# An S4 convolution and GeGLU block on one core: one product for the y tables, weight reads and stores moved, dummy matmuls, another instruction order

## The chip, the cores and the metric

The kernel runs on one core of a Trainium2 chip. The metric is the device time of one execution in microseconds. Three runs of the kernel before gave 823.56, 824.63 and 826.21 us (median 824.63). A separate profiled execution is the source of all trace numbers.

TensorE (PE) multiplies matrices from SBUF into PSUM, VectorE (DVE) and ScalarE (ACT) do elementwise work, and SyncE (SP), ScalarE and GpSimd (POOL) issue DMA transfers. Every engine works through its own instructions strictly in order.

## The reference

All sizes are fixed: 2048 tokens, 448 channels, 256 states per channel, 1792 hidden units.

```python
mod = (_silu(c) @ w_mod).reshape(c.shape[0], 6, 1, -1)
sa, ca, ga, sb, cb, gb = ...
h = _layernorm(x) * (1 + ca) + sa
x = x + ga * _A_ref(h, ...)          # S4 convolution
h = _layernorm(x) * (1 + cb) + sb
x = x + gb * _B_ref(h, ...)          # (gelu(h @ w_gate) * (h @ w_up)) @ w_down
# in _A_ref:
P = jnp.exp(logdA[:, :, None] * l[None, None, :])
K = jnp.einsum("dn,dnl,dn->dl", Cc, P, dB).real
y = irfft(rfft(K) * rfft(u))         # padded to twice the length
y = y + u * Dskip
```

## The kernel before, in words

**Kernel generation and convolution.** The convolution kernel K has 2048 positions for each of 448 channels, each a sum over 256 states of a complex exponential. A position is split into 64 * l1 + l2 (32 values of l1, 64 of l2). For each of 56 steps, 8 channels at a time, small bf16 matmuls with the constant tables `ea` and `rd` form exponents and angles in PSUM. ScalarE turns them into magnitudes (`exps`, tiles `mx` for l1 and `my` for l2) and into sines and cosines (`angles`, tile `fg`, in turns, with a bias tile `halfpi`). VectorE multiplies magnitude and sine or cosine (`mults`): the x factor `tx` in one instruction of 1024 columns (L855), the y factor `ty` in three: the cosine part of 1024 columns (L859), the negated sine part for one half of the l2 values (L862, 512 columns) and the sine part for the other half (L863, 512 columns). TensorE contracts `tx` and `ty` over the states (`kgen`, L886, 64 small matmuls a step). `ktail` evacuates and does the first stage of a Fourier transform (L911).

The input is normalised, transformed in two stages through DRAM (L1040, L1103), multiplied in the frequency domain with the transform of K and transformed back. Channels are taken in three groups (160, 160, 128). `k_fft` handles the first two while kernel generation still runs (L1194, L1198, L1205); `t_fft` the third after the last step (L1276 forward, L1282 and L1285 products, L1292 inverse). The results go to DRAM (L1300) and come back as rows of tokens: early rows of the first two groups (`yi_early`, L1351), last rows of the third (L1362, L1374).

**The passage.** `conv_out` finishes the convolution with small matmuls (L1466 for the early rows, L1471 for the last), adds the residual, computes mean and root (L1478, L1498), normalises (L1512, L1513) and transposes 128 tokens at a time by matmuls with an identity (L1518, L1520). ScalarE copies the result to fp16 (`ht`), VectorE subtracts for the low half (L1528). Four sets of 128 tokens make a block of 512.

**The MLP.** Four blocks. `weight` reads half a weight chunk (512 KB) from `in_wgu` (L1399) and splits it into two fp16 parts (ScalarE L1407, VectorE L1411 and L1412) in a ring of three tiles `wr`; the split chunk is also stored to DRAM (L1421) for the later blocks, which only read it back (`w_load`). The first three of seven chunks belong to the start of the first block (`PRE = 3`). `gate_up` makes the gate and up products of 128 hidden units (20 matmuls at L1594 and four at L1588), gelu on ScalarE (L1601), the product and the fp16 split; it has two pairs of PSUM banks (`pq`). In the first block the first four products are done in two halves of 256 tokens, so that they can start with two of the four sets. `down_first` and `down` make the down product (L1663, L1694, L1754) and store the output.

**Order.** Nothing runs in the order of the source. `Plan.add` records tasks with their engines, planned costs, dependencies and buffers. `Plan.order` then simulates the engines: it takes the engine that could start something first and there the task with the lowest value, either the task's own `v` or a number from the table `PRIO`. Some tasks may go to one of two engines (copies: ScalarE or VectorE), the one that ends first. `HOP` is the planned hand-over time between engines, `RATE` the planned DMA rate, one stream for all queues. The instructions are then written out in this order and stay in it on each engine.

```python
z = add("tys", {"DVE": 1.2}, s - 0.4, fs, [si, y], (), [fb, yb, ty])
...
gate = EV["end"] if cb < PRE else CO[0][1]
hold = [YO[2, 1]] if cb + k < 2 and cb < 2 else YL
t1 = add("w.ld", {"SP": 0.42}, v - 3, ld, [EV["end"]] + hold, [wb], kb=540)
```

`YO[2, 1]` is the store of the second part of the third group; `YL` are all loads of the last rows.

## Time and profile before

| what | value |
|---|---|
| runs | 823.56, 824.63, 826.21 us |
| profiled execution | 822.29 us |
| its span, first to last instruction | 820.5 us |
| TensorE busy | 744.8 us (91%) |
| VectorE busy | 609.2 us (74%) |
| ScalarE busy | 464.4 us (57%) |
| mean granted TensorE clock | 0.972 |
| DMA traffic | 136.78 MB, mean 167 GB/s |

Busy shares are means over stages with different limits; the tables by windows part them. In a row of a timeline or of the chain, the first number is the start in us from the first instruction, the second the duration; a bracket at the end tells how long the engine was idle before it and what ended that. L numbers are lines of the kernel.

### The profile page before, as it was taken

To read this page: it belongs to the slowest core of one execution; us is meant where nothing else is said; L and a number is where in the kernel's file an instruction comes from. 1 tells how busy PE (TensorE), PEld (TensorE's weight loads), DVE (VectorE), ACT (ScalarE), POOL (GpSimd) and SP (SyncE) were. 2 spreads that over 40 slices of the span, in tenths; PEclk is the share of its full clock that TensorE was granted. 3 is DMA by queue.
4 is the path that set the end of the run, shared out by engine and by line. 5 is a ranking of instruction groups with operands and counts; after the bars stand their busy time and mean duration, and the time that the engine had idled before them with its cause. 6 is when DMAs were issued, how large, how long until landed. Compare 5 with 4: busy or idle time off the path is not lost.

```text
span 820.5 us, 19136 instructions
## 1 busy us (share of the span) xinstructions
PE 744.8 (91%) x8172; PEld 455.8 (56%) x8172; DVE 609.2 (74%) x1034; ACT 464.4 (57%) x610; POOL 11.1 (1%) x28
## 2 busy tenths in 40 slices
PE   0787788989899999988689999999999999999997
PEld 0333344443577766678566445444496445954477
DVE  5799999898989999996875783178884655744552
ACT  4598998999899999880245551034332233223320
POOL 1000000000000000001200000000000000000000
PEclk9879999999999999999879999999999999999999
DMA  9644459997967755989769641644416232012101
GB/s 266 161 147 138 116 145 246 282 261 234 221 198 223 224 160 165 295 276 279 242 224 310 234 158 63 162 150 139 135 53 185 77 127 96 24 68 90 45 13 35
DMA packets 92839, 136.78 MB, mean 167 GB/s; under 512 B 22672, under 2 KB 75184, under 8 KB 92754
## 3 DMA queue, kind: packets, MB, share of 16 engines
q1 hardware_dynamic: 86480, 131.02, 52.6%
q10 hardware_dynamic: 5458, 3.12, 1.3%
q8 instruction: 64, 1.05, 0.5%
q0 software_dynamic: 816, 1.42, 0.5%
q14 instruction: 21, 0.17, 0.1%
HBM read 100.42 MB, written 36.01 MB: 166 GB/s over the span
## 4 chain that ended last, share of the span: by engine, by line
PE 62%; ACT 14%; DVE 9%; DMA 8%; issue 5%; SPq 2%; ACTq 0%; DVEq 0%
PE pq L1594 30%; PE pq L1694 8%; PE pd L1663 4%; ACT fg L819 3%; PE kg L886 3%; DMA u_d<-so 2%; PE pg L806 2%; ACT my L793 2%; PE pq L1588 2%; PE pf L1205 2%; PE pf L1103 2%; PE pd L1694 1%; DMA fg<-in_w_mod 1%; DVE ty L859 1%; ACT fg L811 1%
## 5 line engine op out<-in xcount | busy, mean ns | idle before, releaser
L1594 PE MATMUL pq<-ht,wr 128*128 128x512 f16 (+1 forms) x1200 | 248.7, 365 | 0.0
L1594 PEld LDWEIGHTS <-wr 128*128 128x128 f16 x1200 | 114.4, 98 | 128.9 <-issue 12.3
L1608 DVE TENSOR_TENSOR fq<-ge,pq 128x512 f32<-128x512 f32 (+1 forms) x60 | 39.0, 651 | 83.4 <-PE pq L1594 58.5
L1601 ACT ACTIVATE ge<-pq 128x512 f32<-128x512 f32 (+1 forms) x60 | 34.0, 567 | 113.8 <-PE pq L1588 69.4
L1620 ACT ACTIVATE hh<-fq 128x1024 f16<-128x1024 f32 (+1 forms) x49 | 47.2, 964 | 59.9 <-DVE fq L1608 44.5
L886 PE MATMUL kg<-ty,tx 128*32 128x64 f32 x3584 | 63.6, 224 | 13.4 <-DVE ty L863 9.0
L886 PEld LDWEIGHTS kg<-ty,tx 128*32 128x32 f32 x3584 | 54.4, 112 | 32.7 <-DVE ty L863 14.0
L855 DVE TENSOR_TENSOR tx<-mx,fg 128x1024 f32<-128x1024 f32 x56 | 67.3, 1215 | 2.8 <-ACT fg L830 2.8
L1694 PE MATMUL pq<-d,hh 128*128 128x224 f16 x476 | 69.3, 259 | 0.0
L859 DVE TENSOR_TENSOR ty<-my,fg 128x1024 f32<-128x1024 f32 x56 | 67.9, 1216 | 1.7 <-ACT fg L823 1.7
L1694 PE MATMUL pq<-d,hlo 128*128 128x224 f16 x238 | 61.6, 259 | 0.0
L819 ACT ACTIVATE fg<-pg 128x1024 f32<-128x1024 f32 x56 | 57.7, 1032 | 3.5 <-issue 1.5
L793 ACT ACTIVATE my<-pg 128x1024 f32<-128x1024 f32 x56 | 55.9, 1037 | 5.6 <-PE pg L788 5.1
L1623 DVE TENSOR_TENSOR hlo<-fq,hh 128x1024 f16<-128x1024 f32 (+1 forms) x49 | 53.6, 1103 | 3.1 <-ACT hh L1620 3.1
L1694 PEld LDWEIGHTS <-hh 128*128 128x128 f16 x560 | 53.9, 98 | 0.8 <-issue 0.3
L1205 PE MATMUL pf<-q,fc 128*128 128x160 f32 x264 | 41.8, 307 | 0.2
L806 PEld LDWEIGHTS <-lt 64*128 64x128 bf16 x336 | 19.3, 94 | 40.0 <-issue 26.0
L1205 PEld LDWEIGHTS pf<-q,fc 128*128 128x128 f32 x264 | 36.6, 190 | 6.2 <-issue 3.4
L806 PE MATMUL pg<-ea,lt 64*128 64x512 bf16 x168 | 33.1, 387 | 6.7 <-ACT fg L819 5.2
L863 DVE TENSOR_TENSOR ty<-my,fg 128x512 f32<-128x512 f32 x56 | 38.2, 682 | 0.0
L862 DVE SCALAR_TENSOR_TENSOR ty<-my,fg 128x512 f32<-128x512 f32 x56 | 38.1, 681 | 0.0
L911 PE MATMUL kg<-ak,ke 128*64 128x128 f32 x448 | 30.6, 279 | 3.7 <-issue 2.0
(198 smaller groups left out, 1207.2 us busy)
## 6 DMA issues: line engine op xcount, KB each, us to landing
wr<-w_d SPq DMA_DIRECT2D x21, 896.0 KB, 4.6
fc<-in_k_fc SPq DMA_DIRECT2D x20, 576.0 KB, 5.2
u_d<-so SPq DMA_DIRECT2D x32, 224.0 KB, 4.5
w<-in_wgu SPq DMA_DIRECT2D x14, 512.0 KB, 4.1
ui<-u_d SPq DMA_DIRECT2D x10, 672.0 KB, 6.2
w_d<-wr SPq DMA_DIRECT2D x7, 896.0 KB, 7.1
fq<-in_wd SPq DMA_DIRECT2D x14, 448.0 KB, 3.8
us<-uo SPq DMA_DIRECT2D x22, 240.0 KB, 6.5
```

Source lines behind the costliest of these rows:

```text
L793: A.activation(yb.tile.rearrange("p a b c -> p (a b c)"), pb.tile, AF.Exp)
L806: T.matmul(pa[:, nh * 512:nh * 512 + 512], w, x, start=(k == 0), stop=(k == 2))
L819: A.activation(fb.tile[:, 0].rearrange("p x (n k) -> p n x k", n=2), pb.tile.rearrange("p (n x k) -> p n x k", n=2, x=2), AF.Sin, scale=TW ...
L855: V.tensor_mul(tx.tile, xb.tile[:, xm, None, :].to_broadcast([128, 2, 512]), fb.tile[:, :, 0])
L859: V.tensor_mul(ty.tile[:, 1], yb.tile, fy()[:, 1, :, None, :].to_broadcast([128, 16, 2, 32]))
L886: T.matmul(kg[32 * g:32 * g + 32, 2 * (s % 2) + q, :64], tx[:, r, nh, 4 * q + g], ty[:, r, nh, 4 * q + g], start=(r == 0 and nh == 0), sto ...
L1205: T.matmul(pz.tile[:, e % 32 - sl0], fc.tile[:, i, 1 + t], pp.tile[:, t, i], start=(t == 0 and e != 32), stop=(t == 1 and e != 0))
L1594: T.matmul(pb.tile[k][:, ts], wr.tile[:, 4 * lo + t, k, c0:c0 + 128], ht[:, m, ts], start=f % 2 == 0 and i == 0, stop=f % 2 == 1 and i == 9)
L1608: V.tensor_mul(to if half is None else to[:, half:half + 1], *src)
L1620: A.activation(hg.tile[0][:, cb, c], fq.tile[:, c], AF.Copy)
L1623: V.tensor_sub(hg.tile[1][:, cb, c], fq.tile[:, c], hg.tile[0][:, cb, c])
L1694: T.matmul(bank(k)[:, m], x[:, p, q[0], ts], w[:, p, q[1]], start=new and m == 0 and p == 0 and z == 0, skip_group_check=True, stop=i in ( ...
```

## The change

- **One y product.** `ea`, `rd` and the constant `k_one` are changed so that the angles of x and y are shifted by an eighth of a turn and the l2 values lie in two halves. The four products (two halves, sine and cosine) are then plain ones, all done by one VectorE instruction of 2048 columns; the negation goes. `kgen` picks two of the four for each of its two sums, as two runs of 32 columns. The bias and scale of the cosine change sign; ScalarE writes `my` in another order.
- **Weights.** The reads of both halves of the first chunk and of one half of the second (`w.le`) wait only for the end of the kernel generation's buffers and for the load of the residual rows, and come ahead of the row loads on SyncE. The other three (`w.la`) and the stores of the first three chunks (`wr.sa`) are issued by ScalarE and wait for the first root of `conv_out`. Reads of the later four chunks stay on SyncE, behind the last `w.la`.
- **Dummy matmuls** (`spin`), two of 512 columns a task, whose results nobody reads: 5, 5, 4 and 1 tasks after kernel steps 51 to 54 (once the last angles are done), and 18 after the last copies of the third group. Their priority value is 9000, higher than any other, so that they are placed where TensorE has nothing else to start.
- **New order.** Another `PRIO`; a table `PACE` that scales planned costs; hand-over times by pair of engines; a separate planned DMA stream for each issuing queue; some kinds of tasks kept in their own sequence (`INTURN`).

```diff
+PACE = {("anc", "PE"): 0.97, ("ang", "PE"): 0.87, ("bn", "DVE"): 1.12, ...}
-PRIO = {...}
+PRIO = {...}
+    HOPD, HOPB = 0.25, 0.15
+    HOPS = {("PE", "ACT"): 0.2, ("PE", "DVE"): 0.2, ("ACT", "DVE"): 0.04, ...}
+    INTURN = ("ang", "tx", "tyc", "x.mm", "y.mm", "x.exp", "y.exp", "f.ut", ...)
...
-        def fc_():
-            ty.tile = tab.tile([128, 2, 16, 2, 32], FT, name="ty")
-            V.tensor_mul(ty.tile[:, 1], yb.tile, fy()[:, 1, :, None, :].to_broadcast([128, 16, 2, 32]))
-
-        def fs():
-            V.scalar_tensor_tensor(ty.tile[:, 0, :, 0], yb.tile[:, :, 0], -1.0, fy()[:, 0], op0=OP.mult, op1=OP.mult)
-            V.tensor_mul(ty.tile[:, 0, :, 1], yb.tile[:, :, 1], fy()[:, 0])
+        def fy():
+            ty.tile = tab.tile([128, 2, 2, 512], FT, name="ty")
+            V.tensor_mul(ty.tile, yb.tile[:, :, None, :].to_broadcast([128, 2, 2, 512]),
+                         fb.tile[:, None, :, 1].to_broadcast([128, 2, 2, 512]))
...
-                                     ty[:, r, nh, 4 * q + g], start=(r == 0 and nh == 0), stop=(r == 1 and nh == 1),
+                                     ty[:, 0:4:3, nh, 4 * q + g] if r else ty[:, 1:3, nh, 4 * q + g], start=(r == 0 and nh == 0), stop=(r == 1 and nh == 1),
...
+    def spin(n, deps, buf, first, tile_, ops):
+        for k in range(n):
+            def go(k=k):
+                if k == 0:
+                    buf.tile = tile_()
+                w, x, o = ops(buf.tile)
+                for _ in range(2):
+                    T.matmul(o, w, x, start=True, stop=True)
+            first = add("spin", {"PE": 0.43}, 9e3, go, deps + [first], [] if k else [buf], [buf] if k else [])
+        return first
+    SPIN = []
+    for s in range(NSUB - 4, NSUB):
+        SPIN.append(spin((5, 5, 4, 1)[s - NSUB + 4], [FG[NSUB - 1][1], FG[NSUB - 1][2]], Buf("pg"), KGT[s - 1], ...))
...
+        early = cb + k < 2 and cb < 2
-            dma(wb.tile, a["wgu"][cb, :, k])
+            (dma if early or cb >= PRE else adma)(wb.tile, a["wgu"][cb, :, k])
-        hold = [YO[2, 1]] if cb + k < 2 and cb < 2 else YL
-        t1 = add("w.ld", {"SP": 0.42}, v - 3, ld, [EV["end"]] + hold, [wb], kb=540)
+        if early:
+            t1 = add("w.le", {"SP": 0.42}, -1350 + k + 2 * cb, ld, [EV["end"], t_x], [wb], kb=540)
+        elif cb < PRE:
+            t1 = add("w.la", {"ACT": 0.1}, -1350 + k + 2 * cb, ld, [CO["rt", 0]], [wb], kb=540)
+            WT["la"] = t1
+        else:
+            t1 = add("w.ld", {"SP": 0.42}, v - 3, ld, [EV["end"], WT["la"]] + YL, [wb], kb=540)
...
-            dma(w_d[cb], W[0, cb].tile)
+            (adma if cb < PRE else dma)(w_d[cb], W[0, cb].tile)
...
+    spin(18, [EV["ps"], c_ih], Buf("pq"), None, lambda: POOLS["ps"].tile([128, 512], FT, name="pq0"),
+         lambda t: (K2["ih"], K2["ih"][:, None].to_broadcast([128, 4, 128]), t.rearrange("p (a b) -> p a b", b=128)))
```

## The prediction, made before the changed kernel ran

> **What bounds the kernel now.** I read the page's first line, then the busy time of each engine by stage (a table of windows: length, busy time of PE, PEld, DVE, ACT, POOL with instruction counts, then granted clock, DMA share, GB/s), because the mean over the span mixes stages with different limits.

> ```profile
> span 820.5 us, 19136 instructions
> 0.00:41.00 41.00, 17.53 (x48) 8.41 (x50) 27.02 (x66) 21.63 (x33) 3.13 (x14) 0.91 0.76 214
> 41.00:369.60 328.60, 293.79 (x5207) 182.78 (x5208) 310.15 (x489) 303.55 (x387) 0.00 (x0) 0.97 0.71 208
> 369.60:419.70 50.10, 38.07 (x362) 33.46 (x351) 37.09 (x71) 8.97 (x15) 7.94 (x14) 0.83 0.77 238
> 419.70:816.20 396.50, 395.39 (x2574) 231.10 (x2572) 234.18 (x409) 130.23 (x176) 0.00 (x0) 1.00 0.37 120
> ```

> The reader is to see four stages. Start-up (41 us) waits mostly for loads. In the kernel generation and FFTs (328.6 us) VectorE is busy 94.4% and ScalarE 92.4%: two engines bind together, and TensorE has 34.8 us free. In the passage to the MLP (50.1 us) no engine is full, so there a chain of latencies decides. In the MLP (396.5 us) TensorE is busy all but 1.1 us at full clock: nothing that the change touches can shorten it. All gain has to come from the second and third stages.

> How good can the second stage be? Two 50 us stretches of it, the loosest and the tightest:

> ```profile
> 150.00:200.00 50.00, 46.29 (x680) 21.42 (x676) 45.62 (x79) 47.13 (x70) 0.00 (x0) 1.00 0.94 275
> 250.00:300.00 50.00, 48.76 (x899) 36.46 (x900) 48.36 (x70) 48.00 (x55) 0.00 (x0) 1.00 0.66 194
> ```

> The mean of VectorE and ScalarE is 92.8% in the first and 96.4% in the second; over the whole stage it is (310.15 + 303.55) / 2 / 328.6 = 93.4%.

> The third stage I read in the chain of waits that ended last:

> ```profile
> 400.33 0.61 ACT lh L585
> 400.96 3.19 DMA y<-lh
> 404.17 0.65 SPq L1362
> 404.92 3.90 DMA w<-in_wgu
> 413.30 1.65 PE pt L1518 x6
> 419.36 0.41 PE pt L1520 x4
> 419.77 2.29 PE pq L1594 x20
> 424.68 0.67 PE pt L1518 x6
> 425.35 0.37 PE pt L1520 x4
> ```

> The last channel group's result is stored, read back as rows, added, normalised, transposed three times, and only then the first gate matmul starts, at 419.77. Look at 404.92: the rows were issued at 404.17 by SyncE (L1362), a gate weight load directly behind them, and the profile names that load as the one that came last. And look at the transposes: six matmuls take 1.65 us at 413.30, 0.67 us at 424.68. The windows say why (the last three columns again are clock, DMA share, GB/s):

> ```profile
> 400.00:403.00 3.00, 2.28 (x15) 0.79 (x13) 2.85 (x7) 2.22 (x3) 0.60 (x1) 1.00 0.96 301
> 403.00:406.00 3.00, 0.00 (x0) 0.00 (x0) 2.92 (x6) 0.38 (x1) 1.70 (x3) 0.96 0.36 94
> 406.00:409.00 3.00, 0.12 (x2) 0.15 (x4) 1.37 (x3) 0.00 (x0) 0.00 (x0) 0.50 0.92 270
> 416.00:418.00 2.00, 2.00 (x11) 1.45 (x11) 1.75 (x4) 0.39 (x2) 0.00 (x0) 0.50 0.00 0
> ```

> TensorE stops at about 402.3 (2.28 us of work from 400 on), keeps its clock for some 3.5 us (a mean of 0.96 over 403 to 406 puts the fall near 405.8), and then does all of the transposes at half clock.

> **The change part by part.** *One y product.* Each of 56 steps has three VectorE instructions (1024, 512 and 512 columns) and gets one of 2048. The busy times overlap, so starts have to be compared, not durations:

> ```profile
> 282.59 1.21 DVE L859 TENSOR_TENSOR ty<-my,fg 128x1024 f32<-128x1024 f32 x1
> 283.72 1.21 DVE L1198 TENSOR_TENSOR q<-q,pf 128x480 f32<-128x480 f32 x2
> 285.99 0.68 DVE L862 SCALAR_TENSOR_TENSOR ty<-my,fg 128x512 f32<-128x512 f32 x1
> 286.59 0.68 DVE L863 TENSOR_TENSOR ty<-my,fg 128x512 f32<-128x512 f32 x1
> 287.19 0.68 DVE L862 SCALAR_TENSOR_TENSOR ty<-my,fg 128x512 f32<-128x512 f32 x1
> ```

> A 1024-column product holds VectorE for 283.72 - 282.59 = 1.13 us, a 512-column one for 0.60. So 512 columns more cost 0.53, and 2048 cost 1.13 + 2 x 0.53 = 2.19 (at most 2 x 1.13 = 2.26). Before it is 1.13 + 0.60 + 0.60 = 2.33. That saves 0.14 us a step (0.07 at least), 56 x 0.14 = 7.8 us of VectorE (3.9 at least). [...]

> The sines and exponentials keep their shapes (a bias sign, another order of writing): 0. The kernel-generation matmuls read the same 64 columns as two runs of 32; no row shows such a read, TensorE's 34.8 free us could cover 0.62 us a step, and I take 0.

> Is 7.8 us on the path? Only half is VectorE's own: many small copies may go to either engine, so the saving is shared. Busy means fall from 306.85 to (302.35 + 303.55) / 2 = 302.95; at the stage's own 93.4% that makes 324.4 us, a gain of 4.2. If ScalarE alone holds the stage, it is 0; if VectorE alone does, 7.8.

> *New order.* Other planned costs, hand-over times and priorities reorder every engine. No row prices that. The stage could reach its tightest stretch (302.95 / 0.964 = 314.3, a gain of 14.3 with the merge) or fall to its loosest (302.95 / 0.928 = 326.5, a gain of 2.1). I take a third of the way from 93.4 to 96.4%, 94.4%: 320.9 us, a **gain of 7.7** for the stage with the merge; both ends, and the 0 of ScalarE, stay for the range. For start-up and the MLP I take 0; start-up's bound is -2 to +4, a tenth of the 41 us at most.

> *Dummy matmuls.* 18 pairs of 512 columns may run after the last group's copies (400.94), 15 pairs among the last four kernel steps. Their price and the shortened path:

> ```profile
> 445.07 4.42 PE pq L1594 x20
> 413.94 0.69 DVE L1513 SCALAR_TENSOR_TENSOR xn<-xn,rs,rows 128x448 f32<-128x448 f32 x1
> 415.32 0.69 DVE L1513 SCALAR_TENSOR_TENSOR xn<-xn,rs,rows 128x448 f32<-128x448 f32 x1
> 415.62 0.60 ACT L585 ACTIVATE ht<-pt 128x512 f16<-128x512 f32 x1 [2.43 <-PE pt L1520]
> 416.25 0.69 DVE L1528 TENSOR_TENSOR ht<-pt,ht 128x512 f16<-128x512 f32 x1 [0.25 <-ACT ht L585]
> ```

> One costs 0.22 us, so 18 pairs last 8.0 us: with the row products between them they reach from 402.3 to about 411, and the idle time that is left stays under the 3.5 us after which the clock fell. Then a transpose set takes 0.67 + 0.37 = 1.04 us. The second norm ends at 414.63, its set at 415.7, its copy (0.60) at 416.35; VectorE is free of the third norm at 416.0 and does two subtractions of 0.69, until 417.35. That is where the first gate matmul can start: **2.4 us** earlier, bound by VectorE now (bounds 0 to 2.4). A real matmul behind a pair waits up to 0.44 us; the 15 early pairs (6.6 us if all lay on the path) go into TensorE's gaps, and I take 0 for them.

> *Weight loads and stores.* The first three reads move ahead on SyncE, past the early rows and the last constants, right behind the residual rows' load; the other three and three stores leave SyncE and are issued by ScalarE behind the first root. GpSimd's row loads stay.

> ```profile
> yi<-y POOLq DMA_DIRECT2D x6, 32.0 KB, 2.7
> DMA packets 8946, 17.92 MB, mean 249 GB/s; under 512 B 1269, under 2 KB 5781, under 8 KB 8939
> 372.86 11.29 SPq L1351 DMA_DIRECT2D yi<-y  x4
> 376.89 0.69 DVE L1282 TENSOR_TENSOR q<-my,pf 128x512 f32<-128x512 f32 x1 [2.15 <-DMA fg<-in_k_fc]
> 387.90 0.69 DVE L587 COPY lh<-pf 128x512 f32<-128x512 f32 x1 [0.90 <-PE pf L1292]
> 389.24 0.69 DVE L1282 TENSOR_TENSOR q<-my,pf 128x512 f32<-128x512 f32 x1 [0.45 <-PE pf L1276]
> SPq L1399 <- DVE wr L1412: 10.6, 2, 9.8
> SPq L1421 <- DVE wr L1412: 8.0, 2, 7.1
> 389.27 5.65 ACTq L1362 DMA_DIRECT2D yi<-y  x2
> 400.96 0.37 ACTq L1300 DMA_DIRECT2D y<-lh  x1
> ```

> With no weights behind them the last rows should land like GpSimd's, 2.7 us after issue, not about 4.0: **1.3 us** (0 to 1.3). SyncE also stood 11.29 us at the early rows with the constants for the last groups queued behind them; VectorE's holes at 376.89, 387.90 and 389.24 sum to 3.5 us on the chain, and another order may fill them: I take half, **1.75** (0 to 3.5). Against it, the early reads put 1.57 MB in front of those constants, 6.3 us at 249 GB/s; the queue stands there anyway, so I take **-0.5** (0 to -6.3). Six issues of 0.37 us on ScalarE, which is busy 8.97 of 50.1 us in the stage: 0. A store by ScalarE adds a wait: behind it stand the copies, splits and gelus of the first gate products, and TensorE has two pairs of banks before it must wait for a gelu. SyncE stood 10.6 and 8.0 us at exactly those waits for VectorE's splits; freed of them, it only fetches later weights sooner, which full TensorE doesn't need: 0. If the planner places each store behind its split, ScalarE doesn't wait either: 0, up to 18.6.

> Third stage: 2.4 + 1.3 + 1.75 - 0.5 = **5.0**. Sum: 7.7 + 5.0 = 12.7 us.

> **Rivals.** *The order takes most of the idle time.* For it: the 250 to 300 stretch shows 96.4%. Against: buffers and table loads differ by stretch. Then 14.3 + 2.4 + 1.3 + 3.5 + 4 (start-up) = 25.5 us.

> *ScalarE holds the second stage.* For it: 92.4% busy with nothing removed from it. Against: copies can move. Then only 5.0 us are gained; if the early reads cost their 6.3 as well, the change does nothing that can be measured.

> *The clock falls again before the transposes.* The 18 pairs would have to be over by about 409.8, 3.5 us ahead of 413.3; if a third of them run at once in front of the rows, they are. Then the 2.4 us are lost. [...]

> *Slower: ScalarE stands at the stores.* If the order puts stores ahead of their splits, ScalarE stands like SyncE did (and like its own 5.65 us at 389.27), gelus come late, and TensorE, the bound from 419.7 on, loses each of these microseconds. In full: 18.6 us lost against 12.7 won. It decides from 15.2 us on (12.7, and 2.5 for 0.3%).

> **How the numbers follow.** The profiled execution took 822.29 us, 1.79 more than its span; the median shown is 824.63, 2.34 above that. So a gain g gives 824.63 - g. Forecast, 12.7: **811.9** us (chance 0.50; with its bounds 803 to 820). Order takes most: 799.1 (0.20). ScalarE holds: 819.6 (0.17, of which 0.05 within 0.3%, early reads included). Clock falls: 814.3 (0.06). Slower: 830.5 (0.07). 0.3% is 2.5 us, about what a measurement of this kernel can tell from no change: faster 0.50 + 0.20 + 0.12 + 0.06 = 0.88, same 0.05, slower 0.07. The range leaves out the slower case, the no-change case, and a tail beyond the fast rival: 796 to 822.

> **What would show it.** A y product near 2.28 us with the next start about 2.19 later; 41 to 369.6 shrunk by about 8 us with both engines above 94% busy; transposes of 0.67 us and a granted clock of 1.00 from the last group to the gates; no weight load behind the last rows; an MLP of 396 to 397 us. I am wrong if ScalarE's busy share rises while VectorE's falls, if the stage after 369.6 doesn't get shorter, or if the MLP shows gaps in front of gelus.

## The result, and the profile after

The kernel after took 833.18 us (median of 8 runs, 829.08 to 835.54), the kernel before 825.12 us on the same chip (8 runs, 821.77 to 827.44). The ratio is 1.009, with a 95% interval of 1.0068 to 1.0112: **slower by 0.9%**, where 811.9 was predicted. The profiled execution took 835.54 us, its span 833.7.

The four stages of the kernel after, cut at the same events as in the prediction (columns: stretch and its length, busy time of PE, PEld, DVE, ACT, POOL with instruction counts, granted clock, DMA share, GB/s):

```profile
span 833.7 us, 19151 instructions
0.00:41.00 41.00, 17.16 (x40) 7.66 (x40) 28.31 (x70) 16.40 (x29) 3.13 (x14) 0.94 0.79 214
41.00:381.70 340.70, 302.13 (x5226) 187.72 (x5231) 306.86 (x373) 309.90 (x393) 0.00 (x0) 0.95 0.71 203
381.70:434.60 52.90, 46.55 (x402) 34.38 (x400) 37.37 (x73) 9.14 (x15) 7.92 (x14) 0.97 0.76 226
434.60:829.50 394.90, 394.90 (x2573) 230.95 (x2572) 235.05 (x411) 127.99 (x171) 0.00 (x0) 1.00 0.37 118
```

Beside the prediction's table: VectorE has 3.3 us less to do in the second stage (306.86 against 310.15), yet the stage is 12.1 us longer, and both engines stand idle more (VectorE 90.1% busy against 94.4, ScalarE 91.0 against 92.4). ScalarE's work in start-up fell by 5.2 us (16.40 against 21.63) and rose by 6.4 in the stage behind it. The passage grew by 2.8 us. The MLP shrank by 1.6: TensorE has no gap in it any more.

To see where in the long stage, I cut it at four events: the first x product, the first load of u's second transform (SyncE's `ui<-u_d`), the first forward transform of the first channel group's kernels (`pf<-ako`; the expectations below call it the second group's), and the end of the last x product. In the engines' timelines these are, before and then after:

```profile
53.67 1.23 DVE L855 TENSOR_TENSOR tx<-mx,fg 128x1024 f32<-128x1024 f32 x1 [0.47 <-ACT fg L830]
125.45 0.41 SPq L1094 DMA_DIRECT2D ui<-u_d  x1
218.59 1.08 PE L1194 MATMUL pf<-ako,fc 128*128 128x160 f32 x6
367.43 2.35 DVE L855 TENSOR_TENSOR tx<-mx,fg 128x1024 f32<-128x1024 f32 x2
```

```profile
52.01 1.22 DVE L899 TENSOR_TENSOR tx<-mx,fg 128x1024 f32<-128x1024 f32 x1
133.75 0.38 SPq L1134 DMA_DIRECT2D ui<-u_d  x1
232.61 1.08 PE L1250 MATMUL pf<-ako,fc 128*128 128x160 f32 x6
380.44 1.22 DVE L899 TENSOR_TENSOR tx<-mx,fg 128x1024 f32<-128x1024 f32 x1
```

The three stretches between them, before and then after:

```profile
53.70:125.50 71.80, 56.09 (x1018) 30.40 (x1017) 70.69 (x117) 65.42 (x91) 0.00 (x0) 0.95 0.44 129
125.50:218.60 93.10, 84.76 (x1325) 41.22 (x1325) 84.98 (x147) 86.12 (x119) 0.00 (x0) 0.98 0.91 259
218.60:369.80 151.20, 142.86 (x2830) 107.13 (x2828) 143.10 (x201) 141.34 (x165) 0.00 (x0) 1.00 0.72 217
```

```profile
52.00:133.80 81.80, 64.09 (x1150) 35.46 (x1150) 77.02 (x102) 75.72 (x98) 0.00 (x0) 0.87 0.42 125
133.80:232.60 98.80, 86.64 (x1306) 41.10 (x1294) 84.75 (x122) 86.41 (x122) 0.00 (x0) 0.97 0.87 241
232.60:381.60 149.00, 142.04 (x2746) 106.92 (x2750) 137.80 (x137) 136.83 (x160) 0.00 (x0) 1.00 0.77 227
```

So the 13.2 us between the two spans are: start-up -1.7, **first stretch +10**, second +5.7, third -2.2, passage +3.0, MLP -1.7. These are two single profiles. Over all twenty in the table below, the first x product starts between 51.2 and 55.4 us, and with the passage of the kernel after the passage takes 47.9 to 54.3 us, so the differences in start-up and passage lie within the scatter; those in the first two stretches don't.

In the first stretch all three engines do more before u's second transform may begin. TensorE also does it at a lower clock, 0.87 against 0.95 on average. In windows of 3.413 us (last section) the granted clock up to the MLP is 1.00 or 0.50 in each of the two traces, nothing between; by that it is some 21 us at half clock instead of 7: (1 - 0.87) / 0.5 x 81.8 and (1 - 0.95) / 0.5 x 71.8. Of ScalarE's part one group of instructions says what, again before and after (count, then busy us and mean ns):

```profile
L793 ACT ACTIVATE my<-pg 128x1024 f32<-128x1024 f32 x7 | 7.2, 1057 | 0.0
```

```profile
L840 ACT ACTIVATE my<-pg 128x1024 f32<-128x1024 f32 x17 | 17.0, 1045 | 2.7 <-PE pg L835 2.6
```

The kernel before does another seven y exponentials in start-up (6.9 us), where ScalarE has time; the kernel after does one there (1.0 us), so it leaves six of them for the first stretch and adds four.

### The profile page after: what moved, and what is told of

Same layout as the page of the kernel before. It is cut to its first block, busy times and chain, and to the rows that moved or that the text cites. A ratio compares the mean times of both kernels' runs of the same rounds, so it can differ in the third digit from the quotient of the medians.

```text
span 833.7 us, 19151 instructions
## 1 busy us (share of the span) xinstructions
PE 761.1 (91%) x8234; PEld 460.8 (55%) x8238; DVE 608.4 (73%) x927; ACT 463.4 (56%) x607; POOL 11.1 (1%) x28
## 4 chain that ended last, share of the span: by engine, by line
PE 67%; ACT 15%; DVE 6%; DMA 6%; issue 4%; SPq 2%; ACTq 0%; POOL 0%; DVEq 0%; POOLq 0%
PE pq L1657 29%; PE pq L1757 8%; PE pd L1726 4%; PE pg L853 3%; PE kg L926 3%; ACT fg L866 3%; ACT my L840 2%; PE pf L1261 2%; PE pq L1651 2%; PE pf L1348 2%; PE pf L1143 2%; PE pd L1757 1%; ACT mx L822 1%; PE pf L1080 1%; PE pf L1250 1%
## 5 line engine op out<-in xcount | busy, mean ns | idle before, releaser
L903 DVE TENSOR_TENSOR ty<-my,fg 128x2048 f32<-128x2048 f32 x56 | 126.8, 2284 | 2.4 <-PE kg L926 1.5
L853 PE MATMUL pg<-rd,lt 64*128 64x512 bf16 x168 | 34.5, 392 | 0.0
L1143 PE MATMUL pf<-ui,fu 128*128 128x448 f32 x66 | 32.1, 592 | 2.5 <-DVE q L760 1.3
L853 PE MATMUL pg<-ea,rd 64*128 64x512 bf16 x168 | 34.3, 394 | 0.0
```

The lines of the kernel that those rows point to most:

```text
L853: T.matmul(pa[:, nh * 512:nh * 512 + 512], w, x, start=(k == 0), stop=(k == 2))
L903: V.tensor_mul(ty.tile, yb.tile[:, :, None, :].to_broadcast([128, 2, 2, 512]), fb.tile[:, None, :, 1].to_broadcast([128, 2, 2, 512]))
L1143: T.matmul(pb.tile, fu.tile[:, i], ui.tile[:, EORD[e0 + i] % 32 - s0], start=True, stop=True)
```

## The experiments

The planner's order can be written out: the list of tasks of one kernel is replayed in another, so that the order changes and nothing else, or the work and not the order. All kernels come from the source of the kernel after:

```diff
-        for t in self.order():
-            t.fn(t.on) if len(t.eng) > 1 else t.fn()
+        for t, e in written(self):
+            t.fn(e) if len(t.eng) > 1 else t.fn()
```

"Old order" is the list of the kernel before, "new order" that of the kernel after; where two are joined, a task that the first part has issued is skipped in the second. Ratios are against runs of the kernel before on the same chip. The last columns are single profiles: the three stretches, the passage and the MLP, in us.

| kernel | median us | ratio, 95% interval | 1st | 2nd | 3rd | passage | MLP |
|---|---|---|---|---|---|---|---|
| before | 825.12 | 1 | 71.8 | 93.1 | 151.2 | 49.9 | 400.8 |
| after | 833.18 | 1.009 (1.0068 to 1.0112) | 81.7 | 98.9 | 149.1 | 52.9 | 399.1 |
| m1_merge_old_order | 826.21 | 1.0013 (0.9987 to 1.004) | 71.9 | 94.4 | 154.4 | 51.7 | 400.8 |
| a_split_new_order | 837.48 | 1.0129 (1.0085 to 1.0172) | 82.1 | 96.2 | 149.2 | 49.7 | 399.1 |
| h1_old_then_new | 826.03 | 0.9994 (0.997 to 1.0017) | 72.3 | 94.5 | 153.3 | 50.9 | 399.1 |
| h2_new_then_old | 833.82 | 1.0094 (1.0059 to 1.013) | 81.4 | 98.8 | 149.2 | 48.1 | 400.3 |
| old_to_ub_then_new | 831.89 | 1.0085 (1.0055 to 1.0114) | 73.8 | 100.5 | 148.9 | 50.7 | 400.3 |
| new_to_ub_then_old | 834.66 | 1.0111 (1.0078 to 1.0143) | 81.2 | 93.3 | 152.7 | 51.5 | 400.4 |
| old_to_f_then_new | 827.97 | 1.0025 (0.9997 to 1.0052) | 73.1 | 102.0 | 147.3 | 54.0 | 400.8 |
| new_to_f_then_old | 842.56 | 1.0209 (1.0176 to 1.0242) | 82.1 | 98.3 | 155.4 | 53.0 | 401.1 |
| half_y_late_steps | 833.95 | 1.0106 (1.0066 to 1.0146) | 81.4 | 97.6 | 146.9 | 54.3 | 400.2 |
| half_y_early_steps | 835.52 | 1.0122 (1.0084 to 1.0159) | 81.1 | 97.6 | 148.4 | 52.4 | 399.2 |
| half_exp_early_steps | 831.81 | 1.0078 (1.0052 to 1.0105) | 78.8 | 97.3 | 149.3 | 52.3 | 400.3 |
| half_kgen_late_steps | 830.09 | 1.0057 (1.0036 to 1.0077) | 81.6 | 97.7 | 147.1 | 47.9 | 399.1 |
| no_early_dummies | 832.75 | 1.008 (1.0049 to 1.0111) | 81.5 | 96.1 | 148.6 | 51.1 | 399.1 |
| order_searched | 814.65 | 0.9877 (0.9838 to 0.9917) | 66.0 | 97.7 | 148.1 | 51.4 | 398.9 |
| searched_split_y | 818.18 | 0.991 (0.9878 to 0.9942) | 67.1 | 95.1 | 149.0 | 57.6 | 398.8 |
| searched_no_late_dummies | 815.57 | 0.9887 (0.9862 to 0.9913) | 64.9 | 96.3 | 146.8 | 50.8 | 399.8 |
| searched_by_new_costs | 812.77 | 0.9868 (0.9833 to 0.9903) | 67.2 | 96.6 | 147.8 | 48.4 | 398.8 |
| searched_by_old_costs_2 | 816.72 | 0.9898 (0.9876 to 0.9919) | 66.7 | 95.6 | 146.5 | 52.7 | 399.0 |

### The order, or the merged product?

**m1_merge_old_order.** Without `spin` and with the weights as before; the old list, its two y tasks made one.

> The order of the kernel before, written out instruction by instruction, with one change: the y product is merged into one instruction (it stands at the first place of VectorE where, by the plan, both its sine and its cosine are ready). No dummy matmuls, weight reads and stores as before. Theory A (the new order of the kernel-generation stage lengthens it, the merged product itself saves): 2 to 7 us below the kernel before, since 56 x 0.14 = 7.8 us of VectorE's work goes and ScalarE holds part of it. Rival B (one block of 2.2 us on VectorE holds the other engines up): 3 us or more above the kernel before.

No change (1.0013, interval across 1): A's gain isn't there, nor B's loss. **a_split_new_order** puts the three products into the new order:

```diff
-            V.tensor_mul(ty.tile, yb.tile[:, :, None, :]..., fb.tile[:, None, :, 1]...)
+            V.tensor_mul(ty.tile[:, :, 1], yb.tile, fb.tile[:, None, 1, 1]...)
+            V.scalar_tensor_tensor(ty.tile[:, 0, 0], yb.tile[:, 0], 1.0, fb.tile[:, 0, 1], ...)
+            V.tensor_mul(ty.tile[:, 1, 0], yb.tile[:, 1], fb.tile[:, 0, 1])
```

> The kernel after with its own order, but the y product split into three instructions again, next to each other in the place of the merged one. Theory A: 0 to 7 us above the kernel after (8 to 15 us above the kernel before), since the order with its waits stays and VectorE has 7.8 us more to do. Rival B: 5 us or more below the kernel after.

1.0129 against 1.009: some 3 us above the kernel after, the intervals overlapping, and not below it. B is out: the merged block isn't what made the kernel slower. Its third stretch is as long as with the merged product, 149.2 against 149.1.

**h1_old_then_new** and **h2_new_then_old** join the two lists at the passage.

> The order before (with the merged product) up to the end of the third group's inverse products, and from there the order after, with its 18 late dummy pairs, and weight reads and stores by ScalarE. No early dummies. Theory A: 1.5 to 4 us below m1, that is 4 to 10 us below the kernel before: the last rows' transposes run at the full clock, and nothing of the new kernel-generation order is in it. Rival C (the passage and the weights cost more than they bring): at or above m1.

> The reverse: the order after up to the end of kernel generation (merged product, but no early dummies), then the order before, with its weight reads and stores and without any dummy. Theory A: 6 to 13 us above the kernel before. Rival C (the loss lies in the passage, the dummies and the weight moves): within 2 us of m1.

h1 stands at the kernel before, h2 at the kernel after. The loss comes with the order of kernel generation alone; passage, dummies and weight moves together bring nothing that the runs resolve.

### Where in kernel generation?

Two cuts inside the stage, at the first load of u's second transform and at the first forward transform of the kernels, each with old before new and new before old.

> Merged product, no dummies, weights as before. The order before up to the first load of u's second transform (about 125 us), then the order after to the end of kernel generation, then the order before. Whole new kernel-generation order: +8 us (h2), whole old one: +1 us (m1). Theory A1 (the loss arises where the new order leaves VectorE and ScalarE more idle than before, by the two traces +15 us of both engines in 130 to 250 us and +3 us ahead of it): +5 to +8 us against the kernel before. Rival A2 (the new order makes the u path late in the first stretch, 6 us by step 12, and the rest only hands that on): within 3 us of the kernel before.

> The reverse: the order after up to the first load of u's second transform, then the order before to the end. Theory A1: 0 to +3 us against the kernel before. Rival A2: +5 us or more.

> The order before up to the first forward transform of the second kernel group (about 217 us), then the order after to the end of kernel generation, then the order before. Theory A1: about half of the loss arises behind this point (8 of the 20 us of added idle time of the two engines lie in 200 to 250 us): +2 to +5 us. A loss that arises only in u's second transform (130 to 215 us) would leave it within 1.5 us of m1.

> The order after up to the first forward transform of the second kernel group, then the order before to the end. Theory A1: +3 to +6 us, the rest of the +8. A loss that arises only behind this point would leave it within 2 us of the kernel before.

Neither theory holds as put. The new first part alone costs everything (1.0111, as A2 said), and the old first part doesn't save the new second one (1.0085, as A1 said). new_to_f_then_old came out 17 us above the kernel before (1.0209), where A1 put 3 to 6 and its rival within 2; that is 9 us above the whole new order (h2), so a join may cost time of its own, which no run here takes apart. The stretches sort out the rest, as far as single profiles can: each keeps its length with the order it belongs to. The first takes 71.8 to 73.8 us in every kernel with the old order there and 81.1 to 82.1 with the new (78.8 in one that gives ScalarE less to do, below); the second 93.1 to 94.5 old and 96.1 to 98.9 new (old_to_ub and old_to_f are joined at one end of it, so their 100.5 and 102.0 belong to neither); the third 151.2 to 155.4 old and 147.3 to 149.3 new (146.9 and 147.1 in two kernels that have less to do there, below). By the middles of these groups the new order loses about 9 and 4 us in front and wins about 4 behind.

### Does one engine's work set the pace?

Three kernels keep the new order, instruction by instruction, and halve one engine's work in part of the steps:

```diff
+            w = 256 if 27 <= s < 99 else 512
-            V.tensor_mul(ty.tile, ...)
+            V.tensor_mul(ty.tile[..., :w], ...)
```

> The kernel after in its own order, with half of the y product left out from step 27 on: the instruction takes 128x1024 elements, and the kernel-generation matmuls of those steps read the first half of the columns twice (their number stays; the generated kernels of these steps are other numbers). VectorE is relieved of 29 x 1.07 = 31 us behind the first forward transform of the second kernel group. Theory A3 (there TensorE sets the pace, busy 141 of 148 us): 0 to 8 us below the kernel after. Rival V (VectorE sets the pace of kernel generation, as the prediction had it): 20 to 31 us below the kernel after.

> The same with the half left out in steps 0 to 13 alone, 14 x 1.07 = 15 us less for VectorE ahead of the first load of u's second transform. Theory A3 (in the first stretch VectorE sets the pace, and whatever brings u's second transform forward brings the end forward): 6 to 15 us below the kernel after. If the rest of the stage doesn't hang on when that transform begins: less than 3 us.

The windows of the third stretch with the first and of the first stretch with the second:

```profile
231.90:378.80 146.90, 141.22 (x2736) 106.33 (x2736) 108.89 (x137) 135.82 (x159) 0.00 (x0) 1.00 0.77 228
```

```profile
53.80:134.90 81.10, 62.85 (x1117) 34.10 (x1113) 64.22 (x103) 75.24 (x97) 0.00 (x0) 0.87 0.42 126
```

VectorE falls from 138 to 109 us busy in one and from 77 to 64 in the other. The third stretch gets some 2 us shorter in the first of them, the first stretch 0.6 in the second, and neither kernel gets faster (1.0106 and 1.0122 against 1.009, the intervals overlapping). This is the plainest result here: **29 us of VectorE's work can go from the third stretch, or 13 from the first, in this order, and the kernel doesn't get faster.** Rival V is out, and so is A3's claim that VectorE sets the first stretch. Next ScalarE early (`A.activation` on half of the columns, with the halved products) and TensorE late (`for r in range(1 if s >= 27 else 2)` in `kgen`):

> The kernel after in its own order, with half of the y exponentials and of the y products left out in steps 0 to 17 (the generated kernels of these steps are other numbers; the matmuls keep their number). Halving the products alone moved nothing; now ScalarE is relieved of about 17 x 0.45 = 8 us as well, ahead of the first load of u's second transform, where it runs 17 of these exponentials against 7 in the kernel before. Theory S (ScalarE's share placed ahead of u's first transforms makes u late): that load comes 4 to 8 us earlier than at 133.7 us, and the time is 3 to 7 us below the kernel after. Rival (the waits of TensorE's order make u late, whatever the others have to do): within 2 us of the kernel after.

> The kernel after in its own order, with the second half of the kernel-generation matmuls left out from step 27 on (32 instead of 64 a step; the generated kernels of these steps are other numbers). TensorE is relieved of 29 x 0.5 = 15 us behind the first forward transform of the second group. Theory A3 (TensorE sets the pace there, busy 141 of 148 us): 6 to 15 us below the kernel after. Rival (the written order with its chain of waits sets it, no one engine): 0 to 4 us below, as halving VectorE's product there gave.

ScalarE's relief (17 exponentials of 600 instead of 1045 ns, 7.6 us) takes 2.9 us off the first stretch (2.3 to 3.3 against the nine other profiles with this order), and the load comes at 132.7; the whole (1.0078) isn't told apart from the kernel after. TensorE's relief takes 2.1 us off the third, as VectorE's did, and perhaps 2.7 off the whole (1.0057 against 1.009; the intervals overlap). Both lie nearer to the rivals: where it was relieved, no engine sets the pace alone, and work taken from one became idle time there. Not tried were TensorE in the first stretch, ScalarE in the third, and anything in the second but 7 us of VectorE's work (in half_exp_early_steps).

### The dummy matmuls

> The kernel after in its own order without the dummy matmuls of the last four steps. If these stand on the path as the trace of after reads (five ahead of the last transform of the kernels, ten ahead of the third group's first matmul, 2.9 us in all): 1 to 4 us below the kernel after. If they fill gaps, as the prediction had it: within 1 us.

1.008 against 1.009, unresolved. In the trace of the kernel after they do stand on TensorE's way between the last steps and the third group:

```profile
382.55 0.88 PE L926 MATMUL kg<-ty,tx 128*32 128x64 f32 x48
386.34 0.43 PE L926 MATMUL kg<-ty,tx 128*32 128x64 f32 x16 [2.91 <-issue]
386.93 1.78 PE L1188 MATMUL pg<-ea 128*128 128x512 bf16 x5 [0.16 <-issue]
388.64 1.97 PE L951 MATMUL kg<-ak,ke 128*64 128x128 f32 x16
390.55 2.49 PE L1188 MATMUL pg<-ea 128*128 128x512 bf16 x10
393.10 1.60 PE L1332 MATMUL pf<-ako,fc 128*128 128x128 f32 x12
```

Without them the third group's first products start sooner behind the last transform, but the first twelve take 2.93 us, where the kernel before, at a granted clock of 0.50 (375.05 to 378.46), took 2.76:

```profile
386.06 0.37 PE L926 MATMUL kg<-ty,tx 128*32 128x64 f32 x2 [3.27 <-issue]
387.02 1.97 PE L951 MATMUL kg<-ak,ke 128*64 128x128 f32 x16 [0.58 <-DVE ke L946]
389.79 2.93 PE L1328 MATMUL pf<-ako,fc 128*128 128x128 f32 x12 [0.79 <-DVE ako L634]
```

What the dummies cost in delay (2.49 us ahead of the products) they partly give back in clock (1.60 us instead of 2.93, at a granted clock of 1.00 from 390.91 to 394.32).

> order_searched without the late dummy matmuls; the rest of its order stays. The last rows' 15 transposes then run at about 0.37 instead of 0.20 us each as in the kernel before: by the prediction's own step 2.4 us above order_searched. If the path through the passage is VectorE's and the dummies only warm what waits anyway: within 1 us.

0.9887 against 0.9877, unresolved (2.4 us aren't excluded), though the transposes do get slow. Six and four of one set, with and then without the dummies:

```profile
410.42 0.83 PE L1577 MATMUL pt<-ident,xn 128*128 128x128 f32 x6
411.18 0.44 PE L1579 MATMUL pt<-ident,xn 128*64 128x128 f32 x4
```

```profile
404.36 1.65 PE L1577 MATMUL pt<-ident,xn 128*128 128x128 f32 x6 [1.73 <-DVE xn L1572]
405.94 0.70 PE L1579 MATMUL pt<-ident,xn 128*64 128x128 f32 x4
```

### Other orders

A program moved single tasks of h1's list at random and kept what the planner's own costs said was earlier.

> The instructions of h1 (merged product, late dummies, weight reads and stores by ScalarE, no early dummies) in an order found anew, by moving single instructions and keeping what the old planner's costs (0.3 us for each hop between engines, no shortened durations) said was earlier. By that plan u's second transform is first loaded 7 us earlier than in h1 and the second group's forward transforms begin 10 us earlier. Theory A (what counts is when u's path reaches those transforms, and the old costs place it rightly): 8 to 16 us below the kernel before. Rival (the time of kernel generation is set by the sum of VectorE's work, which is the same as in m1 and h1): within 3 us of the kernel before.

0.9877: **1.2% faster than the kernel before**, and by the two ratios (0.9877 / 1.009) 2.1% faster than the kernel after, with the merged product, the late dummies and the weight moves in it. Its first two stretches:

```profile
52.40:118.50 66.10, 53.70 (x940) 30.57 (x939) 62.39 (x85) 61.85 (x90) 0.00 (x0) 0.90 0.49 140
118.50:216.20 97.70, 90.13 (x1457) 43.16 (x1456) 86.82 (x121) 89.17 (x125) 0.00 (x0) 0.97 0.87 238
```

The gain on the kernel before is 5.7 us in the first stretch, where ScalarE does 61.85 us of work against 65.42 before and 75.72 after, and 3 us in the third; the second is 4.6 us longer than before. Seven of the y exponentials are back in start-up and seven are left in the first stretch:

```profile
L840 ACT ACTIVATE my<-pg 128x1024 f32<-128x1024 f32 x7 | 7.2, 1050 | 0.0
```

With the product split again:

> order_searched with the y product split into three again in the place of the merged one: VectorE has 56 x 0.14 = 7.8 us more. If no one engine's work sets the stage: 0 to 4 us above order_searched. If VectorE's does: 6 to 9 us above it.

0.991 against 0.9877, 2.7 us, the intervals overlapping. That is nearer to the first case, but the two intervals don't exclude the 6 us of the second.

Was the new order poor because of the costs that its planner reckons with?

> The same instructions as order_searched, the same start (h1's order), the same number of moves tried; only what judged a move differs: the costs of the planner after (shortened durations, 0.04 to 0.2 us a hop, 0.15 us for a buffer) in place of the planner's before (0.3 us a hop). By the new costs this order ends 4 us ahead of order_searched (792.9 against 797.0) and u's second transform is loaded 1.5 us earlier; by the old costs it ends 18 us behind it (832.8 against 815.1), with that load 6 us later. Theory K (the new costs leave no room for the hops, and that is what made the order after slow): 8 us or more above order_searched, that is -4 to +6 us against the kernel before. Rival (any long search gains, and the order after was merely a poor draw): within 4 us of order_searched's ratio of 0.988.

> A second draw of order_searched: the same search by the old costs with other random moves (815.1 by the old costs, as order_searched). Theory K: within 4 us of order_searched, that is 7 to 14 us below the kernel before. If one draw differs from another by as much as the two costs do: anywhere up to the time of the kernel before.

Not by the costs alone. The search by the new costs gave 0.9868, by the old ones 0.9877 and 0.9898. Theory K falls as put: judged by either costs, a search makes a faster kernel. But all three searches start from h1's order, which has the old kernel generation. Which part of the planner after (its `PRIO`, its costs, the kept sequences) led to its order was not taken apart.

## Why the prediction was wrong

**The step that failed** is "New order", where the prediction took "a third of the way from 93.4 to 96.4%, 94.4%: 320.9 us, a gain of 7.7" (4.2 of it the merge's). The stage got 12 us longer, and with the new order of kernel generation alone (h2) the kernel takes 1.0094 of the time before. Two things were wrong in it. Its bounds came from the loosest and the tightest 50 us of the old order, so that no loss was in them at all; a loose stretch of one order says nothing on how loose another may be. And it took the busy share of two engines for the pace of the stage. Halving VectorE's product, ScalarE's exponentials or TensorE's matmuls in part of the steps moved the time by 0 to 3 us, while reordering the same work moved it by 8 us up and 10 down.

- *One y product.* Sized rightly. In the timeline of VectorE after, two in a row hold it for 134.89 - 130.49 = 4.40 us, 2.20 each, where 2.19 was predicted:

```profile
130.49 4.48 DVE L903 TENSOR_TENSOR ty<-my,fg 128x2048 f32<-128x2048 f32 x2
134.89 0.42 DVE L705 TENSOR_TENSOR q<-q 112x256 f32<-112x256 f32 x1
```

  The 4.2 us that it was to bring are not there in the old order (1.0013); in the two others it is some 3 us, unresolved. With the merged product in the old order the third stretch took 152.7 to 155.4 us instead of 151.2. The sine half now waits with the cosine half, which may be why; that wasn't tested.
- *Start-up and MLP 0.* Start-up came out 1.7 us shorter, but m1, with the old order, shows the same (its first x product starts at 52.07 us), so this isn't put down to the order. Part of the first stretch's 10 us may be the exponentials that moved there: relieving ScalarE by 7.6 us gave some 3 back. The MLP gained 1.7 us (399.1 against 400.8, the medians of the kernels with the new and with the old passage too): TensorE's 1.1 us of gaps went. No gap stands in front of gelus, so the slower rival isn't what happened.
- *Early dummies 0.* The number is right within what the runs resolve, but by luck: they don't go into gaps, they stand on TensorE's way (2.49 us ahead of the third group's products) and give part of it back in clock (1.60 us instead of 2.93 for the first twelve).
- *Late dummies 2.4.* The transposes run at full clock, as predicted (1.00 from 428 to 435, six in 0.91 to 0.94 us, where before they took 1.65), but from the last rows' products to the first gate matmul it is 434.57 - 425.03 = 9.54 us instead of 419.71 - 408.88 = 10.83, so 1.3, not 2.4; VectorE's last norm ends just ahead of the last transposes. Before and then after:

```profile
408.88 0.69 PE L1471 MATMUL pd<-yi,ai 128*64 128x128 f32 x4 [6.60 <-DMA w<-in_wgu]
419.71 2.36 PE L1594 MATMUL pq<-ht,wr 128*128 128x256 f16 x20
```

```profile
425.03 0.66 PE L1533 MATMUL pd<-yi,ai 128*64 128x128 f32 x8
433.37 0.91 PE L1581 MATMUL pt<-ident,xn 128*128 128x128 f32 x6 [0.76 <-DVE xn L1576]
434.57 2.36 PE L1657 MATMUL pq<-ht,wr 128*128 128x256 f16 x20
```

  The other profiles bear it out: 9.5 to 9.6 us in all eight kernels with the new passage (the searched orders aside), 10.4 to 11.0 in five with the old passage. In two more with the old passage (old_to_ub and old_to_f) it is 9.6 and 9.8: there the last six transposes take 0.94 us without any dummy, where the first six take 1.65.
- *Last rows 1.3, VectorE's holes 1.75.* From the last inverse matmul's end to those products it is 425.03 - 417.07 = 7.96 us against 408.88 - 400.30 = 8.58. But that is 7.8 to 8.6 us in the kernels with the new passage and 8.0 to 8.6 in those with the old, so nothing of the 1.3 is told apart; the last rows landed 2.3 to 3.4 us after their issue, before it was 2.3 to 3.9. VectorE's first product of the third group begins 12.6 instead of 7.1 us behind the last x product. This isn't put down to the order either: the same list shows 8.7 us with the product split and 6.7 with half of the late kernel-generation matmuls, and a stop of TensorE (last section) is a good part of the difference. So whether the holes were filled stays open. From that product to the first gate matmul it is 40.1 to 41.3 us with the new passage and 41.6 to 42.8 in the same five with the old: of the 5.0 us of the third stage some 1.5 are there.

**What stays open.** Shown is that the written order of kernel generation made the kernel slower, and, by single profiles, where (first and second stretch). No one engine's work set the pace in the parts that were relieved. Of the 10 us in the first stretch, some 3 came back when ScalarE had less to do. TensorE's lower clock there may be another part. In order_searched the stretch has a clock of 0.90 (13 us at half clock by the same sum) and takes 66.1 us, 5.7 less than the kernel before at 0.95, so a lower clock alone doesn't make it long; what the clock costs there was not measured. Which waits make up the rest, and the 4 to 6 us of the second stretch, was not taken apart.

## What to carry to other kernels

Where several engines are each some 90% busy and hand work round in short pieces, a busy share doesn't say which of them to relieve: halve its work in a copy of the kernel, with the order held fixed, before paying for a saving (here 29 us less for VectorE, busy 92% of the third stretch, took 2 us off it). A new instruction order is a change of its own, to be measured alone, by replaying the old order with the new work and the new order with the old work. And a bound drawn from the old order's rows must leave room for a loss.

## What the runs showed of the hardware that was not expected

TensorE's granted clock did not fall a fixed time after its last work, as the prediction took it with its 3.5 us. In order_searched the dummies end at about 402.87 and the next matmul starts at 405.40; the clock (third column from the end) falls at 405.43, some 2.6 us after the last work. It also fell at 88.00, with no pause of TensorE longer than 1.01 us in the 3.41 us ahead:

```profile
84.59:88.00 3.41, 1.94 (x16) 0.67 (x18) 3.41 (x4) 3.41 (x6) 0.00 (x0) 1.00 0.75 201
88.00:91.41 3.41, 3.41 (x107) 2.81 (x110) 3.32 (x6) 3.41 (x6) 0.00 (x0) 0.50 0.20 73
402.02:405.43 3.41, 0.88 (x6) 0.26 (x5) 1.40 (x4) 0.00 (x0) 0.11 (x1) 1.00 0.82 232
405.43:408.84 3.41, 3.41 (x18) 1.69 (x20) 2.54 (x9) 0.48 (x2) 0.00 (x0) 0.50 0.35 100
87.63 0.39 PE L835 MATMUL pg<-ea,lt 64*128 64x512 bf16 x2 [1.01 <-ACT mx L822]
```

So the first dummies did not carry the clock to the transposes in order_searched; the row products and the dummies among them ran at a clock of 0.50 from 405.43 to 408.84, with TensorE busy throughout, and it was 1.00 again from there, ahead of the transposes at 410.42. In the kernel after, where dummies reach to 424.92 and the row products start at 425.03, it stayed (1.00 in every window from 422 to 435).

TensorE also stopped inside a step's matmuls near the end of kernel generation, for 2.91 us after and 3.27 without the early dummies, with nothing in the profile that it waited for. VectorE, which copies the result of these matmuls next, stands idle ahead of that copy for 4.01 us after and 4.22 without the early dummies; the list of the kernel after shows 2.25 us there with the product split, and 0.17 with half of the late kernel-generation matmuls. The kernel before has a stop of 1.99 us ahead of the last transform (372.92), of which VectorE's copies, until 371.49, may explain 0.6. The share of busy DMA is 0.98 or more in each microsecond from 383 to 387 in the kernel after; whether that is the reason wasn't tried.
